# Attention into four experts on one core: order of the first chunks, places of the second batch's attention, and a last block in two column halves

## The chip, the cores and the metric

The kernel runs on one core of a Trainium2 chip. The metric is the time of one execution on the device in microseconds. The core's engines are TensorE (PE: matrix products into PSUM; PEld: its loading of the stationary operand), VectorE (DVE), ScalarE (ACT), GpSimd (POOL) and SyncE (SP). Here POOL and SP also issue the DMAs.

## The reference

Pooled attention for 8 batches of 8 heads, 576 tokens and 64 columns per head, then four experts on the 4608 tokens:

```
k_p, v_p = mean of k and v over groups of 8 tokens          # 72 keys per head
attn     = softmax(q @ k_p^T / sqrt(64))                    # per head
x        = attn @ v_p, heads side by side                   # [4608, 512]
p        = domain_probs / (sum over experts + 1e-9)
out      = sum over e of p[:, e] * (relu(x @ w1[e]) @ w2[e])  # w1 512x1024, w2 1024x512
```

All operands of the matrix products are bf16.

## The kernel before

**Chunks and steps.** The tokens are worked on in nine chunks of 512. Chunk c below 8 holds the first 512 tokens of batch c; chunk 8 holds the last 64 tokens of all batches. For every chunk there are four experts, so there are 36 steps (c, e), numbered s = 4c + e. In step s the hidden layer of (c, e) is made ("up") while the output of the step before, s - 1, is accumulated ("down").

**Forms of a step.** Some steps multiply plainly: `up_plain` makes 8 row blocks of the hidden layer, each with four matmuls of 512 columns into a PSUM bank `h_ps` and a relu on ScalarE; `down` makes four output blocks r of 128 tokens, each with 8 matmuls of 512 columns into a bank `o_ps`, and `merge` adds the block, times its probability, to `acc` (on VectorE, or on ScalarE for e = 0). The others use a Strassen form: seven half-size products in place of eight (`up_seven`, products of 256 columns into banks `g_ps`, with sums and relus on ScalarE (L691, L698) and VectorE (L695)); from step 7 on `up_down` uses it for up and down together. The Strassen forms need combinations of w1 (`combine_w1`), w2 (`combine_w2`), x (`forms_of`) and of the hidden layer (`sums_of`), most of them made on VectorE. Some overwrite a block that the plain form still needs, so they may only run once the last plain user is through.

**Order.** Every engine's queue is in the order in which the Python code runs; nothing is reordered by a scheduler. A counter `at` counts points: each call of `point()` runs what the dictionary `placed` holds for that number. `between(j, n)`, with j in 0, 1 and n in 0 to 3, makes one point, then a quarter of one half of the previous step's down products (3, 4, 5 and 4 matmuls), then pops one entry of the queue `forms_due` and makes a second point. A step without `up_down` so has 16 points; step 4 begins at point 64.

**Attention.** The attention of batch 0 (`attention_first`) runs at the start. That of batch 1 (`second_attention`) is placed at the points 42 to 64: its keys are folded on VectorE, transposed on TensorE (`second_keys`, L319), its queries are transposed in two halves (`second_queries`, L329), then come four groups of scores (`scores`, L272, followed by an exp on ScalarE, L276), the folding of the values, and four groups of contexts (`context`, L395), each followed on VectorE by a reciprocal and a division (`divide`, L376 and L377) and on SP by a DMA transpose (`turn`, L416) into `xT`. From batch 2 on `attention(c)` places the same work during chunk c for batch c + 1, with c = 1 for batch 2, and keys and queries are turned by DMA transposes (`keys`, `queries`). In `loads_wait` POOL waits for the transposed keys before it issues further loads.

**PSUM.** There are three pools: `psum_a` holds one tile of two banks, used in turn by scores, contexts and the transposes named above; `psum_h` and `psum_o` hold three banks each. A tile can be written again once its last reader is through.

**Places that the change touches.** `turn_here` (L423) turns x of batch 0 on TensorE: it takes a tile of `psum_a` for r = 0 and for r = 2, and r = 1 and 3 use that tile's other half. In step 4, (1, 0), the up products of chunk 1 are plain and alternate with the down products of (0, 3) in the second half of the step (L1006 to L1010). At the very end the step after the last one runs the down products of (8, 3), each block followed by an addition (L872) and, since chunk 8 gathers two batches per block, two stores of 64 rows (L888).

Of the kernel before, what the change touches and what calls it, by code (L numbers as in the profile page):

```python
# [13 lines left out]
BF16 = mybir.dt.bfloat16  # L14
F32 = mybir.dt.float32
# [3 lines left out]
def kernel(  # L19
# [10 lines left out]
    nc = tc.nc  # L30

    B, H, S, D = q.shape
# [78 lines left out]
    def load_q(b):  # L111
        q_sb = qpool.tile([P, H, NR, D], BF16, name="q_sb")
        nc.gpsimd.dma_start(
            out=q_sb[:].rearrange("p h r d -> p h (r d)"),
            in_=q[b, :, 0:NT, :].rearrange("h (p r) d -> p h (r d)", r=NR),
        )
        raws[("q", b)] = q_sb
# [22 lines left out]
    def load_v(b):  # L140
        load_kv(b, v, "vraw")
# [281 lines left out]
    def turn_here(b, r):  # L423
        if r == 0:
            state[("xT", b)] = xpool.tile([P, KC, NT], BF16, name="xT")
        if r % 2 == 0 or b:
            state["xt_ps"] = psum_a.tile([P, 2, KC, P], BF16, tag="a", name="xt_ps")
        xt_ps = state["xt_ps"][:, r % 2]
        flat = state.pop(("x", b, r))[:].rearrange("p a h d -> p (a h d)")
        for kc in range(KC):  # L430
            nc.tensor.transpose(xt_ps[:, kc, :], flat[:, kc * P:(kc + 1) * P], ident[:])
        nc.scalar.copy(out=state[("xT", b)][:, :, r * P:(r + 1) * P], in_=xt_ps)  # L432

    def rem_queries(i):
        q_rem = q_rems.pop(i)
# [80 lines left out]
    def second_attention():  # L516

        lo, hi = halves

        return {  # L520
            42: [lambda: fold_keys(1, lo)],
            44: [lambda: fold_keys(1, hi), lambda: load_k(2)],
            47: [second_keys],
            50: [lambda: second_queries(0)],
            51: [lambda: second_queries(1), lambda: load_q(2), lambda: load_q_rem(2)],
            53: [lambda: scores(1, 0)],
            55: [lambda: scores(1, 1)],
            56: [lambda: fold_values(1, lo)],
            57: [lambda: scores(1, 2)],
            58: [lambda: fold_values(1, hi)],  # L530
            59: [lambda: scores(1, 3)],
            60: [lambda: context(1, 0), lambda: turn(1, 0)],
            61: [lambda: context(1, 1), lambda: turn(1, 1)],
            62: [lambda: context(1, 2), lambda: turn(1, 2)],
            63: [lambda: context(1, 3), lambda: turn(1, 3)],
            64: [lambda: load_v(2)],
        }

    def attention(c):

        lo, hi = halves
        b = c + 1
        plan = {}

        def add(n, *what):
            plan.setdefault(n, []).extend(what)

        if c % 2:
            i = c // 2
            q_at = 15 if b < B else 2  # L550
            for n, piece in zip((0, 8, 11, 12), (rem_queries, rem_scores, rem_context, rem_turn)):
                add(q_at + n, lambda piece=piece: piece(i))
        parts = forms_of(b, nc.gpsimd)
        add(25, *parts)
        if b == B:
            return plan
        more, far = b + 1 < B, b + 2 < B
        if c == 1:
            add(0, lambda: queries(b), *key_parts(b)[:2])
            add(1, *key_parts(b)[2:])  # L560
            add(1, lambda: keys(b), lambda: loads_wait(b))
            add(1, lambda: (load_q(b + 1), load_q_rem(b + 1)))
            for pair in range(NPAIR):
                add(7 + pair, lambda pair=pair: scores(b, pair))
            for n, part in enumerate(value_parts(b)):
                add(6 + n, part)
            mixed = (11, 12, 13, 14)
        else:
            for pair in range(NPAIR):
                add(2 + 2 * pair, lambda pair=pair: scores(b, pair))  # L570
            for n, part in enumerate(value_parts(b)):
                add(4 + n, part)
            mixed = (9, 11, 12, 19)
        for n, r in zip(mixed, range(NR)):
            add(n, lambda r=r: context(b, r))
            add(n + 1, lambda r=r: turn(b, r))
        if more:
            add(4, lambda: load_half(b + 1, k, "kraw", 0))
            add(11, lambda: queries(b + 1))
            add(8, lambda: load_half(b + 1, k, "kraw", 1))  # L580
            add(16, *key_parts(b + 1))
            add(21, lambda: load_half(b + 1, v, "vraw", 0))
            add(27, lambda: load_half(b + 1, v, "vraw", 1))
            add(24, lambda: keys(b + 1))
        if far:
            add(28, lambda: (load_q(b + 2), load_q_rem(b + 2)))
        return plan
# [259 lines left out]

    def down(c, e, j, n):

        first = (0, 3, 7, 12, 16)  # L850
        for at in range(first[n], first[n + 1]):
            r, fc = 2 * j + at // FCH, at % FCH
            if fc == 0:
                sums[r] = psum_o.tile([P, DM], F32, name="o_ps")
            nc.tensor.matmul(  # L855
                sums[r][:], lhsT=hidden[(c, e)][:, fc, r * P:(r + 1) * P], rhs=w2_bf[:, e, fc, :],
                start=(fc == 0), stop=(fc == FCH - 1),
            )
            if fc == FCH - 1:
                if held is not None and r == NR - 1:  # L860
                    held.append(lambda: merge(c, e, r, sums[r]))
                else:
                    merge(c, e, r, sums[r])

    def merge(c, e, r, o_ps):
        prob = p_all[:, c * NR + r, e:e + 1]
# [10 lines left out]
            return  # L877
        store(c, r)

    def store(c, r):  # L880
        dst = accs[(c, r)][:]
        if c < B:
            rows = out[c * S:c * S + NT, :].rearrange("(p r) d -> p r d", r=NR)
            nc.sync.dma_start(out=rows[:, r, :], in_=dst)
        else:
            for bb in range(2):
                at = (2 * r + bb) * S + NT
                nc.sync.dma_start(out=out[at:at + REM, :], in_=dst[bb * REM:(bb + 1) * REM])  # L888

    zeros = x_rem[:, 0]  # L890
    pool_map = x_rem[0:FR, 1, 0:FT * SP].rearrange("p (r j) -> p r j", r=FT)
# [1 line left out]
    with tc.manual_schedule(engines={ENG.PE, ENG.DVE, ENG.Activation, ENG.Pool, ENG.SP}):  # L893
# [52 lines left out]
        for s in range(len(steps) + 1):  # L946
# [17 lines left out]
            if s == 1:  # L964
                w, u, x = combine_w2(0), combine_w1(0), forms_of(0)
                forms_due.extend([lambda w=w, u=u, n=n: (w[n](), u[n]()) for n in range(3)])
                forms_due.extend(nothing[:1] + combine_w1(2))
                for part in x[:3]:
                    part()
            elif s == 2:  # L970
                x[3]()
                forms_due.extend(nothing + combine_w1(3))
            elif s == 4:
                v2, x = combine_w2(1), forms_of(1)
                forms_due.extend(v2[:2] + combine_w1(1))
                forms_due.extend([lambda: (x[0](), x[1]()), lambda: x[2]()])
            elif s == 5:
                x[3]()
                forms_due.extend(u[3:] + nothing[:2] + combine_w2(2))
            elif s == 6:  # L980
                v3 = combine_w2(3)
                forms_due.extend(nothing[:1] + v3[:1] + nothing[:2] + v3[1:])
            elif s == 7:
                forms_due.extend(nothing[:1] + v2[2:3] + nothing[:3] + v2[3:])
            elif s == 8:
                forms_due.extend(nothing[:1] + w[3:])
            elif s == E * B + 1:
                reload_w2(E - 1)
            for j in range(2):
                if not live:  # L990
                    for n in range(4):
                        between(j, n)
                elif s == 0:
                    for i in range(4):
                        up_half(j, i)
                        if j == 0 and i in (1, 2):
                            turn_here(0, i + 1)
                        if j == 0 and i == 2:
                            norm_probs()
                        between(j, i)  # L1000
                elif s == 1:
                    for n in range(4):
                        between(j, n)
                    for n in range(4):
                        up_plain(c, e, [4 * j + n])
                elif s == E:  # L1006
                    for n in range(4):
                        between(j, n)
                        if j:
                            up_plain(c, e, [2 * n, 2 * n + 1])  # L1010
                elif splits(*steps[s - 1]):
                    up_down(c, e, j, *steps[s - 1])
                else:
                    up_seven(c, e, j, lambda n: between(j, n))
# [30 lines left out]
```

## Time and profile before

| what | value |
|---|---|
| median of three runs | 506.51 us (506.37 to 507.28) |
| profiled execution | 508.62 us |
| its span on the core | 506.9 us |
| TensorE busy | 494.3 us, 98% |
| VectorE, ScalarE, GpSimd busy | 70%, 57%, 35% |
| granted TensorE clock, mean | 0.997 |
| DMA | 41.90 MB, near full in the first 75 us, far less later |

The profile comes from one execution. A row of a timeline gives start and duration in us, engine, line, operation, output and inputs, and in brackets the idle time of the engine before it with the instruction that ended it. Matmuls overlap, so a row of several matmuls lasts about 0.16 us longer than the time until the next row can start. A granted clock of 0.50 means half speed of TensorE.

### The profile page before, as it was taken

What the parts mean: (1) busy time and instruction counts of PE and PEld (TensorE: products, weight loads), DVE (VectorE), ACT (ScalarE), POOL (GpSimd) and SP (SyncE); (2) the same over time, 40 slices, a digit from 0 to 9 for tenths busy, and PEclk for the clock granted to TensorE, in tenths of its full rate; (3) what the DMA queues carried; (4) which work ended last, traced back from release to release, by engine and by line L of the source; (5) the groups of instructions that cost most, each with busy time, mean ns of one, the idle gap of its engine ahead of it and who ended that gap; (6) DMA issues with size and microseconds to landing.
All of it is one profiled execution on the core that took longest, in us unless ns stands there. A gap on an engine that the chain in (4) does not pass through costs nothing.

```text
span 506.9 us, 10946 instructions
## 1 busy us (share of the span) xinstructions
PE 494.3 (98%) x4483; PEld 392.6 (77%) x4483; DVE 355.5 (70%) x650; ACT 287.6 (57%) x531; POOL 179.7 (35%) x165
## 2 busy tenths in 40 slices
PE   8899889999999999999999999999999999999996
PEld 3656544567788888888888888888888888888883
DVE  2363879678777776777777777777877767776674
ACT  2554352745676557665766576556655565556650
POOL 8372102135622671266226722661115111512110
PEclk9899999999999999999999999999999999999999
DMA  9999998893747346844773286343200110012003
GB/s 130 206 206 204 203 142 155 127 88 38 83 106 98 48 47 121 118 48 44 125 107 51 21 124 118 50 46 63 64 16 18 43 43 12 2 43 63 2 1 83
DMA packets 83506, 41.90 MB, mean 83 GB/s; under 512 B 46576, under 2 KB 78832, under 8 KB 83456
## 3 DMA queue, kind: packets, MB, share of 16 engines
q0 software_dynamic: 42112, 22.91, 35.4%
q1 hardware_dynamic: 41344, 18.29, 17.8%
q8 instruction: 35, 0.57, 0.5%
q14 instruction: 15, 0.12, 0.1%
HBM read 45.69 MB, written 9.44 MB: 109 GB/s over the span
## 4 chain that ended last, share of the span: by engine, by line
PE 90%; DVE 5%; DMA 1%; ACT 1%; issue 1%; POOL 1%; POOLq 0%; ACTq 0%
PE g_ps L647 38%; PE u_ps L769 35%; PE o_ps L855 8%; PE h_ps L665 3%; PE two L272 2%; PE h_ps L678 2%; PE two L395 1%; DMA q_sb<-in_q_dram 1%; DVE H_sb L695 1%; DVE x_tok L377 1%; DVE acc L872 1%; DVE acc L753 0%; ACT xT L432 0%; PE two L452 0%; POOL H_sb L107 0%
## 5 line engine op out<-in xcount | busy, mean ns | idle before, releaser
L647 PEld LDWEIGHTS <-w_bf 128*128 128x128 bf16 x1848 | 177.5, 98 | 27.8 <-issue 2.5
L753 DVE SCALAR_TENSOR_TENSOR acc<-u_ps,p_all,acc 128x512 f32<-128x512 f32 (+1 forms) x204 | 121.3, 594 | 77.0 <-ACT u_ps L806 72.7
L715 POOL TENSOR_TENSOR h_s<-H_sb,h_s 128x1024 bf16<-128x1024 bf16 x29 | 61.4, 2119 | 231.1 <-DVE h_s L714 231.1
L647 PE MATMUL g_ps<-xT,w_bf 128*128 128x256 bf16 x928 | 130.0, 273 | 0.0
L647 PE MATMUL g_ps<-xf,w_bf 128*128 128x256 bf16 x792 | 109.8, 272 | 0.6 <-ACT g_ps L790 0.4
L691 ACT COPY r<-g_ps 128x512 f32<-128x512 f32 x140 | 82.1, 586 | 46.4 <-PE g_ps L647 41.8
L695 DVE CUSTOM_DVE_ANT_0 H_sb<-g_ps,r 128x512 bf16<-128x512 f32 x140 | 96.4, 689 | 12.8 <-ACT r L691 8.2
L769 PEld LDWEIGHTS <-H_sb 128*128 128x128 bf16 x928 | 86.8, 98 | 18.2 <-DVE H_sb L713 4.7
L769 PE MATMUL u_ps<-w_bf,H_sb 128*128 128x256 bf16 x696 | 95.3, 273 | 0.4 <-DVE H_sb L713 0.3
L698 ACT ACTIVATE H_sb<-g_ps 128x512 bf16<-128x512 f32 x124 | 74.1, 597 | 20.6 <-PE g_ps L647 20.6
L769 PEld LDWEIGHTS <-h_s 128*128 128x128 bf16 x696 | 68.1, 98 | 7.9
L790 ACT COPY g_ps<-g_ps 128x512 f32<-128x512 f32 x58 | 33.1, 570 | 65.3 <-PE g_ps L647 65.3
L769 PE MATMUL u_ps<-w_t,h_s 128*128 128x256 bf16 x464 | 69.6, 273 | 0.0
L855 PE MATMUL o_ps<-w_bf,H_sb 128*128 128x512 bf16 x224 | 54.7, 379 | 0.0
L806 ACT COPY u_ps<-u_ps 128x256 f32<-128x256 f32 x58 | 20.7, 357 | 32.8 <-PE u_ps L769 32.6
L855 PEld LDWEIGHTS <-H_sb 128*128 128x128 bf16 x224 | 21.7, 98 | 18.9
L769 PE MATMUL u_ps<-w_t,H_sb 128*128 128x256 bf16 x232 | 35.0, 273 | 0.0
L769 PE MATMUL u_ps<-w_bf,h_s 128*128 128x256 bf16 x232 | 34.8, 273 | 0.0
L276 ACT ACTIVATE expT<-two 72x1024 bf16<-72x1024 f32 x28 | 28.5, 1017 | 4.0 <-PE two L272 4.0
L377 DVE TENSOR_TENSOR x_tok<-two,inv 128x512 bf16<-128x512 f32 x32 | 22.1, 692 | 1.1
L808 DVE TENSOR_SCALAR acc<-u_ps,p_all 128x512 f32<-128x512 f32 x14 | 10.5, 751 | 16.8 <-ACT u_ps L806 16.8
L794 ACT COPY u_ps<-u_ps 128x256 f32<-128x256 f32 x58 | 21.1, 363 | 0.0
(116 smaller groups left out, 433.0 us busy)
## 6 DMA issues: line engine op xcount, KB each, us to landing
out_dram<-acc SPq DMA_DIRECT2D x32, 256.0 KB, 2.4
w_bf<-in_moe_w_dram POOLq DMA_DIRECT2D x17, 256.0 KB, 10.1
w_bf<-in_moe_w_dram POOLq DMA_DIRECT2D x4, 1024.0 KB, 17.4
q_sb<-in_q_dram POOLq DMA_DIRECT2D x7, 512.0 KB, 10.0
raw_kv<-in_k_dram POOLq DMA_DIRECT2D x10, 288.0 KB, 6.6
raw_kv<-in_v_dram POOLq DMA_DIRECT2D x10, 288.0 KB, 6.6
raw_kv<-in_k_dram POOLq DMA_DIRECT2D x2, 576.0 KB, 14.8
w_t<-in_v_dram POOLq DMA_DIRECT2D x2, 576.0 KB, 13.7
```

The source lines that it names most:

```text
L276: nc.scalar.activation(out=state[("expT", b)][:, 2 * pair:2 * pair + 2].rearrange("j h r s p -> j s (h r) p"), in_=two[0:SP].rearrange("j ...
L377: nc.vector.tensor_tensor(out=x_tok[:], in0=c_ps[:, :, :, 0:D], in1=inv[:].unsqueeze(3).to_broadcast([P, 2, NPAIR, D]), op=ALU.mult,)
L647: nc.tensor.matmul(bank[:, t, :], lhsT=w1_bf[:, e, block, kc, lo:lo + P], rhs=x[:, kc, :], start=(first and t == 0 and kc == 0), stop=(t = ...
L691: nc.scalar.copy(out=r[:], in_=ps[:])
L695: nc.vector._custom_dve(TENSOR_ADD_SAT, out=out, in0=ps[:], in1=r[:], s0=BIG, s1=0.0)
L698: nc.scalar.activation(out=out, in_=ps[:], func=ACT.Relu)
L715: lambda: nc.gpsimd.tensor_sub(out=s4, in0=a12, in1=s2),
L753: nc.vector.scalar_tensor_tensor(out=acc, in0=ps, scalar=prob, in1=acc, op0=ALU.mult, op1=ALU.add,)
L769: nc.tensor.matmul(out, lhsT=lhs[0][:, lhs[1] + f, lhs[2]], rhs=rhs[0][:, rhs[1] + f, rhs[2]], start=(start and f == 0), stop=(f == FCH // ...
L790: nc.scalar.copy(out=s[:], in_=g[:])
L794: nc.scalar.copy(out=two[:, lo], in_=one[:, lo])
L855: nc.tensor.matmul(sums[r][:], lhsT=hidden[(c, e)][:, fc, r * P:(r + 1) * P], rhs=w2_bf[:, e, fc, :], start=(fc == 0), stop=(fc == FCH - 1),)
```

## The change

The change has six parts.

1. `turn_here`: each r takes a tile of one bank's half; r = 1 takes it from `psum_o`, the others from `psum_a`.
2. `second_attention`: keys of batch 1 move from point 47 to 49, the second half of the queries from 51 to 52 with the loads of q that follow, the first three groups of scores one point later, the contexts from 60, 61, 62, 63 to 61, 63, 65, 68, and the load of v of batch 2 to 69.
3. `attention(1)`: the transposes and folds of batch 2 begin two places (four points) later, its scores, values and contexts one place later.
4. Step 4: all down products of its second half come first, then all eight plain row blocks.
5. `forms_due`: the four combinations of w2 of expert 1 move from steps 4 and 7 to steps 7 and 8; in step 4 the combinations of w1 of expert 1 and the forms of x are queued later and two at a time.
6. End: the last block of (8, 3) is made in two halves of 256 columns, each with its own addition and store, and the stores of chunk 8 become one DMA per block (or half) in place of two.

```diff
     def turn_here(b, r):
...
-        if r % 2 == 0 or b:
-            state["xt_ps"] = psum_a.tile([P, 2, KC, P], BF16, tag="a", name="xt_ps")
-        xt_ps = state["xt_ps"][:, r % 2]
+        pool, tag = ((psum_o, "o_ps") if r == 1 else (psum_a, "a"))
+        xt_ps = pool.tile([P, KC, P], BF16, tag=tag, name="xt_ps")
...
-            47: [second_keys],
+            49: [second_keys],
             50: [lambda: second_queries(0)],
-            51: [lambda: second_queries(1), lambda: load_q(2), lambda: load_q_rem(2)],
-            53: [lambda: scores(1, 0)],
-            55: [lambda: scores(1, 1)],
-            56: [lambda: fold_values(1, lo)],
-            57: [lambda: scores(1, 2)],
-            58: [lambda: fold_values(1, hi)],
+            52: [lambda: second_queries(1), lambda: load_q(2), lambda: load_q_rem(2)],
+            54: [lambda: scores(1, 0)],
+            56: [lambda: scores(1, 1), lambda: fold_values(1, lo)],
+            58: [lambda: scores(1, 2), lambda: fold_values(1, hi)],
             59: [lambda: scores(1, 3)],
-            60: [lambda: context(1, 0), lambda: turn(1, 0)],
-            61: [lambda: context(1, 1), lambda: turn(1, 1)],
-            62: [lambda: context(1, 2), lambda: turn(1, 2)],
-            63: [lambda: context(1, 3), lambda: turn(1, 3)],
-            64: [lambda: load_v(2)],
+            61: [lambda: context(1, 0), lambda: turn(1, 0)],
+            63: [lambda: context(1, 1), lambda: turn(1, 1)],
+            65: [lambda: context(1, 2), lambda: turn(1, 2)],
+            68: [lambda: context(1, 3), lambda: turn(1, 3)],
+            69: [lambda: load_v(2)],
...
         if c == 1:
-            add(0, lambda: queries(b), *key_parts(b)[:2])
-            add(1, *key_parts(b)[2:])
-            add(1, lambda: keys(b), lambda: loads_wait(b))
-            add(1, lambda: (load_q(b + 1), load_q_rem(b + 1)))
+            add(2, lambda: queries(b))
+            add(2, *key_parts(b)[:2])
+            add(3, *key_parts(b)[2:])
+            add(3, lambda: keys(b), lambda: loads_wait(b))
+            add(3, lambda: (load_q(b + 1), load_q_rem(b + 1)))
             for pair in range(NPAIR):
-                add(7 + pair, lambda pair=pair: scores(b, pair))
+                add(8 + pair, lambda pair=pair: scores(b, pair))
             for n, part in enumerate(value_parts(b)):
-                add(6 + n, part)
-            mixed = (11, 12, 13, 14)
+                add(7 + n, part)
+            mixed = (12, 13, 14, 15)
...
     def down(c, e, j, n):
-        first = (0, 3, 7, 12, 16)
+        if (c, e) == (B, E - 1) and j and n:
+            if n == 1:
+                for lo in (0, TH):
+                    last_half(c, e, NR - 1, lo)
+            return
+        first = (0, 3, 7, 12, 16) if (c, e) != (B, E - 1) or j == 0 else (0, FCH)
...
+    def last_half(c, e, r, lo):
+        o_ps = psum_o.tile([P, DM], F32, tag="o_ps", name="o_ps")
+        cols = slice(lo, lo + TH)
+        for fc in range(FCH):
+            nc.tensor.matmul(
+                o_ps[:, 0:TH], lhsT=hidden[(c, e)][:, fc, r * P:(r + 1) * P],
+                rhs=w2_bf[:, e, fc, cols], start=(fc == 0), stop=(fc == FCH - 1),
+            )
+        dst = accs[(c, r)][:, cols]
+        add(dst, p_all[:, c * NR + r, e:e + 1], o_ps[:, 0:TH])
+        nc.sync.dma_start(out=rem_rows(r)[:, :, cols], in_=dst)
...
+    def rem_rows(r):
+        return out.rearrange("(b s) d -> b s d", s=S)[2 * r:2 * r + 2, NT:S]
...
-            for bb in range(2):
-                at = (2 * r + bb) * S + NT
-                nc.sync.dma_start(out=out[at:at + REM, :], in_=dst[bb * REM:(bb + 1) * REM])
+            nc.sync.dma_start(out=rem_rows(r), in_=dst)
...
             elif s == 4:
-                v2, x = combine_w2(1), forms_of(1)
-                forms_due.extend(v2[:2] + combine_w1(1))
-                forms_due.extend([lambda: (x[0](), x[1]()), lambda: x[2]()])
+                x = forms_of(1)
+                u1 = combine_w1(1)
+                forms_due.extend(nothing + [
+                    lambda: (u1[0](), u1[1]()), lambda: (u1[2](), u1[3]()), lambda: x[0](),
+                    lambda: (x[1](), x[2]()),
+                ])
...
             elif s == 7:
-                forms_due.extend(nothing[:1] + v2[2:3] + nothing[:3] + v2[3:])
+                v2 = combine_w2(1)
+                forms_due.extend(nothing[:1] + v2[:1] + nothing[:3] + v2[1:2])
             elif s == 8:
-                forms_due.extend(nothing[:1] + w[3:])
+                forms_due.extend(nothing[:1] + w[3:] + v2[2:3] + nothing[:2] + v2[3:])
...
                 elif s == E:
                     for n in range(4):
                         between(j, n)
-                        if j:
-                            up_plain(c, e, [2 * n, 2 * n + 1])
+                    if j:
+                        up_plain(c, e, range(FCH))
```

More of the change, by code (lines that the diff above doesn't have):

```diff
@@ L431, in turn_here @@
             nc.tensor.transpose(xt_ps[:, kc, :], flat[:, kc * P:(kc + 1) * P], ident[:])
-        nc.scalar.copy(out=state[("xT", b)][:, :, r * P:(r + 1) * P], in_=xt_ps)
+        nc.scalar.copy(out=state[("xT", b)][:, :, r * P:(r + 1) * P], in_=xt_ps[:])
     def rem_queries(i):
```

## The prediction

> **What bounds the kernel now.** I read the page first: engine shares, then the chain that ended last.
>
> ```profile
> PE 494.3 (98%) x4483; PEld 392.6 (77%) x4483; DVE 355.5 (70%) x650; ACT 287.6 (57%) x531; POOL 179.7 (35%) x165
> ...
> PE 90%; DVE 5%; DMA 1%; ACT 1%; issue 1%; POOL 1%; POOLq 0%; ACTq 0%
> ```
>
> TensorE carries nine tenths of the chain, and from 95 us to the tail the waits name four idle gaps of TensorE, none over 0.3 us. The change neither adds nor removes matrix work to speak of, so it can only win or lose in places where TensorE waits. The timeline of TensorE, searched for idle time, gives these places before 95 us; the number in brackets is the idle time and who ended it:
>
> ```profile
> 18.07 0.38 PE L431 MATMUL xt_ps<-ident,x_tok 128*128 128x128 bf16 x4 [0.41 <-ACT xT L432]
> ...
> 56.02 0.30 PE L319 MATMUL kpt_ps<-ident,kp 72*128 72x72 bf16 x4 [0.98 <-DVE kp L207]
> ...
> 60.33 0.61 PE L329 MATMUL qt_ps<-ident,q_sb 128*128 128x128 bf16 x8 [0.30 <-DVE qT L333]
> ...
> 72.35 0.43 PE L395 MATMUL two<-vp,expT 72*128 72x65 bf16 x8 [0.61 <-DVE x_tok L377]
> ...
> 73.84 0.43 PE L395 MATMUL two<-vp,expT 72*128 72x65 bf16 x8 [0.63 <-DVE x_tok L377]
> ...
> 75.30 0.43 PE L395 MATMUL two<-vp,expT 72*128 72x65 bf16 x8 [0.16 <-DVE x_tok L377]
> ```
>
> All of them lie where the diff works: transposes of batch 0 (18 us), keys and queries of batch 1 (56 to 60), its contexts (70 to 75). The last place is the end, where TensorE is done at 502.30 and the rest is one addition and two stores:
>
> ```profile
> 497.92 6.29 SPq L888 DMA_DIRECT2D out_dram<-acc  x8
> ...
> 502.33 0.75 DVE L872 SCALAR_TENSOR_TENSOR acc<-o_ps,p_all,acc 128x512 f32<-128x512 f32 x1 [0.98 <-PE o_ps L855]
> ```
>
> The windows view adds the granted clock, 0.50 from 19.0 to 22.4 us, where 16 products of 256 columns take 0.213 us each and not 0.109.
>
> **What the Trainium skill says.** "TensorE: Matmul & The Clock Gate", section "What's actually happening": after an idle window of about 3.4 us the clock is halved, and the windows run freely. The trace agrees (3.4 us at half clock after a stretch with many gaps). "PSUM — Partial Sum Buffer", section "Engine vs sequencer instructions": VectorE and ScalarE queues are strictly first in, first out. The trace agrees: at 58.40 two relu sums (L695) run back to back, the first behind two weight combinations. "DMA: Bandwidth & Descriptors", section "Anatomy of one DMA": about 2 us of a DMA are fixed. The trace agrees: 128 KB stores land 2.2 us after issue, 256 KB ones 2.3 to 2.4.
>
> **The change part by part.** Rows used: four 256-column products 0.44, a down product 0.216, a group of scores 0.34 plus 0.10 of delay ahead of it (61.65 + 5 x 0.216 = 62.73, but it starts at 62.82), a group of contexts 0.26, from one context to the next when VectorE is free 1.46 (73.84 to 75.30).
>
> *Start.* `turn_here` r=1 gets a bank of its own. Its four transposes start at 17.66, after the contexts, and not at 18.07; the first up product then starts at 18.70, not 19.13. **-0.4**. For r=2 and 3 nothing changes: they shared a bank before, and still take turns in one.
>
> *Keys and queries of batch 1.* `second_keys` moves behind eight products (0.87) and three down products (0.65), so to 54.75 + 1.52 - 0.4 = 55.9. The folded keys are ready at 55.96 - 0.4 = 55.56, so the 0.98 is gone. What is late next is the load of q of batch 1: issued at 35.97, it lands 21.8 later, at 57.8. TensorE would reach `second_queries` at 55.9 + 0.28 + 0.87 = 57.0 and waits until 57.85. Then 0.44 + 4 x 0.216 gives 59.15, eight products 60.02, where the second half needs the first half's copy. VectorE has no gap here: relu sums (58.40 + 1.28) and copy (0.68), all 0.4 earlier, end at 59.9. So the second half runs 60.02 to 60.46, and the five down products after it start at 60.46, not 61.65: **-1.19 with the start, -0.79 without**.
>
> *Contexts of batch 1.* Before, start minus nominal end of the work ahead: 0.30 (the last exp held the bank), 0.78, 0.78, 0.33 = 2.19. After, walking on from 60.46: scores 0 waits 0.1 for the query copy; scores 2 and 3 now have only 0.86 of products between them, and the 1.02 us exp plus the copy of g put ahead of it on ScalarE hold the bank, 0.43; each context has 1.1 to 1.6 of products to the next one, but VectorE also runs a merge (0.66) or relu sum (0.65) ahead of the divide: 0.44, 0.20, 0.42. Sum 1.59, **-0.60**.
>
> *25 down products, then all 32 up products.* Same matrix work, **0**. The up products need the four turned pieces of x: they landed at 77.6 to 79.2 before, behind the load of v of batch 2 (69.98 + 7.1 = 77.1). Now the last is issued near 76.8 and lands near 79.2, while TensorE gets there at 81.0. ScalarE's relu takes 0.60 per 0.865 of matmul. On SP's queue one output store now stands ahead of the transpose of q of batch 2 and a second one ahead of that of its keys (all four came after it before); by my walk the keys go out at 81.3 (81.75 before), and they are needed at 89.1. POOL's order is unchanged.
>
> *Next step (c=1, e=1).* Its first half now holds four exps, not three: four of 1.02, three copies of 0.59, one relu 0.60, two merges 0.69 = 7.8 of 8.3 us on ScalarE. The last exp ends about 97.5 where the first context of batch 2 is reached at 97.25: 0.3. Contexts 2 and 3 of batch 2 are now two points apart with a weight combination (0.68) ahead of the divide: 2.95 against 2.64, 0.3. Nothing there waited before. **+0.6**.
>
> *w2 combinations of expert 1* go from steps 4 and 7 to 7 and 8; used in step 10. Step 8 gets two VectorE instructions of 0.68; after the first VectorE had 2.3 us idle (to 143.54), the second delays the sums of the next step by 0.6. **0**, at most 0.3.
>
> *Tail.* 24 products of 512 and 16 of 256 take the same time. The last addition is 128x256: about 0.45 (1.01 for two at 494.02), not 0.75. The last block then goes out by one store, not two: the second was issued at 503.62. The final issue comes at 502.32 + 0.03 + 0.45 = 502.8: **-0.8**. Cover: the first half's addition and issue end at 502.4.
>
> Sum: -1.19 - 0.60 + 0 + 0.6 + 0 - 0.8 = **-2.0**. The profiled execution took 508.62 (span 506.90 and 1.72 around it), so 506.6 for the like. The three runs shown have a median of 506.51, 2.1 below the profiled one; the difference of 2.0 is carried to it: **504.5**.
>
> Bounds from both sides. Start with keys and queries: -0.2 if the loads, which run 90% of the time here, end the waits; -1.4 if q lands early. Contexts: 0 if merges fall badly, -1.5 if no divide is late. Next step: 0 to +1.2. Tail: -0.5 to -1.0. I take the walk's values since each comes from rows next to the place.
>
> **Rivals.** *Loads take the gain.* w2 of expert 2 lands at 54.6 and is wanted at 55.2, q lands at 57.8 and is wanted at 57.0: earlier TensorE meets them. For: DMA is busy throughout these 40 us. Against: VectorE sets the second half of the queries anyway. With -0.2 there and +1.2 in the next step: -0.2 - 0.6 + 1.2 - 0.8 = -0.4, 506.1.
>
> *The half-clock window goes away.* With 0.4 us less idling before 19 us the window may count as busy. 16 products x (0.213 - 0.109) = 1.7 more: 502.8. For: the idling is just what is shortened. Against: 0.4 of 3.4 us is little, and the runs shown may already lack it.
>
> *Slower: keys of batch 2 land late.* They are the one transfer that now waits behind two stores on SP, and scores of batch 2 stop TensorE for it. Price: in the trace a transpose that met a large load took 13.0 us to land (q at 96.47), against 2.7 for these keys. 81.3 + 13 = 94.3 against 89.1 is 5.2 lost: 509.7. It turns the sign to slower when the landing passes 92.1. Against: POOL's next loads wait for exactly this transpose (`loads_wait`), and v of batch 2 has landed by then.
>
> That the change doesn't do what it says is excluded: in the built program the 25 down products stand in a row ahead of the 32 up products, and the contexts are spread.
>
> **Numbers.** Forecast 0.60 (0.56 faster, 0.04 within), loads 0.16 (0.02 and 0.14), clock 0.14, late keys 0.10. A measurement of this kernel can tell about 0.2%, 1.0 us, from no change. Faster 0.72, same 0.18, slower 0.10. Range 502.7 to 506.2, from the clock rival to the loads rival; what lies outside is mainly the late keys.
>
> **What would show it.** Right: no wait at the key transposes; `second_queries` starts near 57.8; four context waits below 0.5 each; up products from about 81 to 88; a wait near 0.3 at the first context of batch 2; last store issued 0.5 after TensorE ends. Wrong: TensorE waiting for a DMA before the scores of batch 2; new gaps after 95 us; a different stretch at clock 0.5.

## The result and the profile after

The changed kernel takes 522.40 us (median of 4 runs, 522.03 to 523.06) and the kernel before 506.45 us beside it (506.37 to 507.28): a ratio of 1.031, with a 95% interval of 1.0295 to 1.033. The forecast was 504.5. The profiled execution took 522.65 us, with a span of 521.0. One of the 21 executions with two store queues (below), the profiled one, took 1024.85 us and is left out, so that tail is read from the timeline of the last experiment.

First the page of the changed kernel, engine shares and chain. TensorE is busy about as long as before (493.0 us), but its share has fallen from 98 to 95%, and 5% of the chain are now DMA:

```profile
PE 493.0 (95%) x4491; PEld 392.4 (75%) x4491; DVE 355.0 (68%) x651; ACT 287.2 (55%) x531; POOL 179.6 (34%) x165
...
PE 83%; DMA 5%; DVE 5%; ACT 2%; issue 1%; POOL 1%; POOLq 0%; ACTq 0%
```

Next the timeline of its end (start, duration, engine, line; in brackets the idle time and who ended it). The last down products run from 493.26, the last addition starts at 500.39 and takes 0.48, as the prediction said. Then comes what it did not say: the two issues of the last block take 10.00 us together on SP's queue, where eight took 6.29 before, and the span ends at 521.0, more than 20 us after TensorE:

```profile
493.26 5.34 PE L858 MATMUL o_ps<-w_bf,H_sb 128*128 128x512 bf16 x24
...
495.97 5.05 SPq L905 DMA_DIRECT2D out_dram<-acc  x3
...
500.39 0.48 DVE L751 SCALAR_TENSOR_TENSOR acc<-o_ps,p_all,acc 128x256 f32<-128x256 f32 x1 [0.39 <-PE o_ps L873]
501.12 10.00 SPq L879 DMA_DIRECT2D out_dram<-acc  x2
```

And the DMA view of the changed kernel from 503 to 517 us, fourteen microseconds in which no other engine computes (queue: packets, MB, share of the 16 DMA engines):

```profile
DMA packets 423, 0.71 MB, mean 51 GB/s; under 512 B 8, under 2 KB 147, under 8 KB 423
...
q1 hardware_dynamic: 423, 0.71, 13.2%
```

Four blocks of 256 KB leave at 51 GB/s, with 13.2% of the DMA engines busy: two of 16 are 12.5%. At that rate the whole 1.05 MB takes 20.6 us; in the kernel before it leaves from 498 us to the end at 506.9 with 50.8% of the DMA engines busy. That is where the loss lies.

Ahead of the tail the idle places of TensorE are these (timeline of the changed kernel, up to 75 us):

```profile
18.83 1.91 PE L676 MATMUL h_ps<-xT,w_bf 128*128 128x256 bf16 x16 [0.41 <-ACT xT L431]
...
54.31 0.81 PE L858 MATMUL o_ps<-w_bf,H_sb 128*128 128x512 bf16 x3 [0.39 <-DMA w_bf<-in_moe_w_dram]
...
57.04 0.62 PE L329 MATMUL qt_ps<-ident,q_sb 128*128 128x128 bf16 x8 [0.78 <-DMA q_sb<-in_q_dram]
...
71.50 0.43 PE L395 MATMUL two<-vp,expT 72*128 72x65 bf16 x8 [0.26 <-DVE x_tok L377]
...
74.45 0.43 PE L395 MATMUL two<-vp,expT 72*128 72x65 bf16 x8 [0.16 <-DVE x_tok L377]
```

The wait for the keys (0.98) is gone, those at the contexts have shrunk, and two waits for loads have come. The 16 products at 18.83 take 1.91 and not 3.48: this execution has no half-clock stretch, which was worth 1.57. From one landmark of TensorE to the next, both profiled executions:

| stretch, by the start of | before | after | change |
|---|---|---|---|
| first down products of step 2 | 42.60 | 40.74 | -1.86, of which -1.57 is the half-clock stretch |
| down products behind the queries of batch 1 | 61.65 | 59.68 | -0.11 more |
| products behind the 32 up products of (1,0) | 90.27, with 0.44 of scores ahead | 87.02 | -0.84 more |
| first row of 12 down products in step 7 (chain view) | 121.17 | 118.75 | +0.39 |
| last down products | 495.22 | 493.26 | +0.46 |
| end of the span | 506.9 | 521.0 | +16.06 |

The sum is 14.1, the difference of the spans; without the half-clock stretch it is 15.7, next to the 15.95 between the medians. So the body (all that lies ahead of the last down products) gains 0.4 us without that stretch, and the tail loses 16.1.

### The profile page after: what moved, and what is told of

It reads as the page before. It is cut to its first block, busy times and chain, and to the rows that moved or that the text cites. A ratio compares the mean times of both kernels' runs of the same rounds, so it can differ in the third digit from the quotient of the medians.

```text
span 521.0 us, 10962 instructions
## 1 busy us (share of the span) xinstructions
PE 493.0 (95%) x4491; PEld 392.4 (75%) x4491; DVE 355.0 (68%) x651; ACT 287.2 (55%) x531; POOL 179.6 (34%) x165
## 4 chain that ended last, share of the span: by engine, by line
PE 83%; DMA 5%; DVE 5%; ACT 2%; issue 1%; POOL 1%; POOLq 0%; ACTq 0%
PE g_ps L645 35%; PE u_ps L767 33%; PE o_ps L858 6%; DMA q_sb<-in_q_dram 5%; PE h_ps L663 2%; PE two L272 2%; PE two L395 1%; PE h_ps L676 1%; DVE acc L751 1%; DVE H_sb L693 1%; DVE x_tok L377 1%; DVE w_bf L636 0%; ACT r L689 0%; PE o_ps L873 0%; ACT xT L431 0%
## 5 line engine op out<-in xcount | busy, mean ns | idle before, releaser
L767 PEld LDWEIGHTS <-H_sb 128*128 128x128 bf16 x928 | 86.7, 98 | 18.3 <-DVE H_sb L711 4.9
L858 PE MATMUL o_ps<-w_bf,H_sb 128*128 128x512 bf16 x216 | 52.9, 379 | 0.4 <-DMA w_bf<-in_moe_w_dram 0.4
L858 PEld LDWEIGHTS <-H_sb 128*128 128x128 bf16 x216 | 20.6, 98 | 18.6 <-issue 1.2
```

What stands on the lines that cost most here:

```text
L767: nc.tensor.matmul(out, lhsT=lhs[0][:, lhs[1] + f, lhs[2]], rhs=rhs[0][:, rhs[1] + f, rhs[2]], start=(start and f == 0), stop=(f == FCH // ...
L858: nc.tensor.matmul(sums[r][:], lhsT=hidden[(c, e)][:, fc, r * P:(r + 1) * P], rhs=w2_bf[:, e, fc, :], start=(fc == 0), stop=(fc == FCH - 1),)
```

## Experiments

Two theories for the tail. **Few engines**: the store `rem_rows(r)` has two steps (batches) in its outermost dimension, and so runs on two DMA engines. **Column halves, or size**: the pieces of 1 KB rows, or 256 KB to two separate places, are slow by themselves. The median of the kernel before was 506.9, 507.13 and 506.91 beside the three sets of runs.

**Two stores again (first set).** In both places of the store:

```diff
-        nc.sync.dma_start(out=rem_rows(r)[:, :, cols], in_=dst)
+        for bb in range(2):
+            at = (2 * r + bb) * S + NT
+            nc.sync.dma_start(out=out[at:at + REM, cols], in_=dst[bb * REM:(bb + 1) * REM])
```

> The changed kernel, but each of the last chunk's blocks goes out by two stores of 64 rows again (one for each batch); the column halves of the last block stay, as two stores of 64x256 each. Theory 'few engines': the merged store, whose outermost DRAM dimension has two steps, is moved by two of the 16 DMA engines at 51 GB/s, and four of them (1 MB) take 20.5 us; with 64 rows outermost each store lands in about 2.2 us, TensorE's end is followed by about 3.3 us, and the time is 505.5 to 506.3 us, 16 us below the changed kernel. Rival 'column halves': the last block's pieces of 1 KB rows are what is slow, or the last additions; then the time stays above 515. Rival 'body': the time was lost before the tail; then it stays at 520 or more.

Measured: 507.46 us, ratio 1.0005 (0.9995 to 1.0015). Fifteen of the sixteen microseconds are back with the column halves still there; it is the merged store. The time is 1 us above the range expected, though. In the timeline of this kernel ten issues stand in SP's queue, and the last ends at 502.81, 2.2 us after the last addition (500.58):

```profile
495.68 4.56 SPq L909 DMA_DIRECT2D out_dram<-acc  x6
...
500.10 0.48 DVE L751 SCALAR_TENSOR_TENSOR acc<-o_ps,p_all,acc 128x256 f32<-128x256 f32 x1 [0.39 <-PE o_ps L873]
500.33 2.48 SPq L881 DMA_DIRECT2D out_dram<-acc  x4
```

**The kernel before with the merged store.**

```diff
-            for bb in range(2):
-                at = (2 * r + bb) * S + NT
-                nc.sync.dma_start(out=out[at:at + REM, :], in_=dst[bb * REM:(bb + 1) * REM])
+            rows = out.rearrange("(b s) d -> b s d", s=S)[2 * r:2 * r + 2, NT:S]
+            nc.sync.dma_start(out=rows, in_=dst)
```

> The kernel before, with one edit: the last chunk's blocks go out by one store of 2x64x512 each. Everything else, the order of the products and the one last block of 512 columns included, is as before. Few engines: four stores of 256 KB at 51 GB/s are 20.5 us from the first one's issue (near 488 to 489 us as in the changed kernel, or as much later as the kernel before's tail is), so 520 to 524 us. Column halves or body: 506 to 507.

Measured: 523.82 us, ratio 1.033 (1.0306 to 1.0346). This one edit makes the whole loss, without any of the rest. The issues by line (shortest/median/longest ns) grow from 0.5 to 4.9 us as the queue behind the two engines fills:

```profile
L887 SPq DMA_DIRECT2D out_dram<-acc x4: 520/1126/4895, 497.4 to 502.5; - x4
```

**The same bytes, the dimensions exchanged** ("rows first" below).

```diff
-        return out.rearrange("(b s) d -> b s d", s=S)[2 * r:2 * r + 2, NT:S]
+        return out.rearrange("(b s) d -> s b d", s=S)[NT:S, 2 * r:2 * r + 2]
```

> The changed kernel, with one store for a block as it is, but the two outer dimensions of its DRAM side exchanged: 64 rows by 2 batches by 512. Bytes, rows of 2 KB and number of stores are the same; two tokens' rows within a block are stored at each other's places, so this part of the output is permuted. Few engines: what counts is the outermost dimension, so 64 puts the store on 16 engines: it lands in 2.3 to 2.5 us and the time is 505.0 to 506.0, a little under the form with two stores. Rival 'size': a store of 256 KB to two separate places is slow whatever the order of its dimensions: 520 or more.

Measured: 505.55 us, ratio 0.9969 (0.9962 to 0.9977). One store for a block, 256 KB, 2 KB rows, two places: all as in the changed kernel, and 16.9 us faster. Size is out. DMA view of this kernel, from 493 to 507 us in 40 slices (busy tenths of the 16 engines, then GB/s), and its landing times:

```profile
DMA  0000000000089101970029970900000000000000
GB/s 0 0 0 0 0 0 0 0 0 0 0 316 398 35 0 59 421 269 0 0 94 410 366 255 12 339 24 0 0 0 0 0 0 0 0 0 0 0 0 0
...
out_dram<-acc SPq DMA_DIRECT2D x3, 256.0 KB, 2.4
out_dram<-acc SPq DMA_DIRECT2D x2, 128.0 KB, 2.1
```

**Four batches in a block.**

```diff
-        return out.rearrange("(b s) d -> b s d", s=S)[2 * r:2 * r + 2, NT:S]
+        b, s = 4 * (r // 2), NT + 32 * (r % 2)
+        return out.rearrange("(b s) d -> b s d", s=S)[b:b + 4, s:s + 32]
```

> The changed kernel, with one store for a block, but the block goes to 32 rows of four batches (4x32x512) in place of 64 rows of two; the remainder rows of the output are permuted by this. Few engines: four engines at 25.6 GB/s each, 102 GB/s; 256 KB take 2.56 us, four blocks 10.2 us from the first issue. The blocks come every 1.73 us, so each is late by 0.83 us more than the one ahead, and the end is about 2.56 us of the last pair after a queue of some 2.5 us: 507 to 511 us, far below the changed kernel and above the form on 16 engines. Rival 'any leading dimension under 16 is equally slow' (one engine pair, whatever the shape): 522. Rival 'size': 522 as well.

Measured: 512.7 us, ratio 1.011 (1.009 to 1.0125). The DMA view from 500 to 508 us has twice the rate and twice the share of the changed kernel, which fits four engines in place of two (no view names single engines, so their number is read from rate and share):

```profile
DMA packets 460, 0.80 MB, mean 100 GB/s; under 512 B 13, under 2 KB 125, under 8 KB 460
...
q1 hardware_dynamic: 460, 0.80, 26.3%
```

The time is above my range. The rate expected holds, but only from about 500 us; ahead of that the first store had moved at 13 to 50 GB/s for 2.6 us. Why one such store alone is below the rate of its engines stays open.

**The body alone (second set):** `down` and `store` as in the kernel before, the rest as changed.

> The changed kernel with the tail of the kernel before: one last block of 512 columns, two stores for each of the last chunk's blocks, as before. This is the body of the change alone. By the traces (start -0.4, keys and queries -0.1, contexts -0.8, next step +0.4, two weight combinations in step 8 +0.46, that is -0.45 in all) against those runs of before that have no half-clock stretch (506.7): 506.1 to 506.4. By the prediction's own terms for the body (-1.2): 505.5. Rival 'the late stores hid more': above 507.

Measured: 506.54 us, ratio 0.998 (0.9973 to 0.9988). That is 0.6 below the median of before in this set (507.13), and 0.2 below the lower of the two groups in which its runs lie (see below; 506.72). It is 0.1 above the range that the traces gave; their -0.4 is nearer than the prediction's own -1.2 for the body.

**The turns of batch 0 alone:** the kernel before with the new `turn_here`.

> The kernel before with only the edit in the turns of batch 0: the second turned block has a bank of its own. Theory 'half clock': the runs of before fall into two groups, 506.3 to 507.2 and 507.8 to 508.5, and the upper one (a third of them) has the half-clock stretch after 19 us, worth 1.7; the shorter gaps take it away in every run, so that the runs form one group at 506.0 to 506.7, and the profile shows the 16 products at 18.5 us in 1.9 us. Rival: the edit wins its 0.4 only, with a third of the runs still 1.7 higher, and medians differ by 0.4. Second rival: the loads at 54 and 57 us take up the 0.4: 506.6 with one group.

Measured: 506.78 us, ratio 0.9988 (0.998 to 0.9996). The 52 runs of before in this set lie in two groups, 29 from 506.27 to 507.28 and 23 from 507.80 to 508.47; the 21 runs of this kernel lie in one, from 506.00 to 507.42. All but one of the upper group had a granted clock of 0.997 or less, which is what 3.4 us at half clock leave of 505 us; in the lower one two of 29 had. The medians of the groups are 1.3 apart (508.03 and 506.72), a little less than the stretch's 1.57; why is open. In the timeline of the kernel with this edit alone the 16 products take 1.91 us, and the later waits are those of before, for VectorE and not for loads:

```profile
18.32 1.91 PE L677 MATMUL h_ps<-xT,w_bf 128*128 128x256 bf16 x16 [0.41 <-ACT xT L431]
...
53.76 0.30 PE L319 MATMUL kpt_ps<-ident,kp 72*128 72x72 bf16 x4 [0.97 <-DVE kp L207]
...
58.08 0.61 PE L329 MATMUL qt_ps<-ident,q_sb 128*128 128x128 bf16 x8 [0.30 <-DVE qT L333]
```

With the edit the upper group is gone. That its runs had the half-clock stretch is inferred from the clocks (though two of the 21 runs, at 506.45 and 506.53, also have 0.997) and from the timelines: the two without the edit, before and before with the merged store, take 3.48 and 3.49 us for the 16 products, the ten with it 1.91 each. The edit's 0.4 does not show against the lower group (506.72 to 506.78), and the second rival does not explain it: TensorE waits for no load at 54 or 57 us in this timeline. Where the 0.4 goes stays open.

**The w2 combinations put back** to steps 4 and 7, on top of the kernel with rows first (edit: the branches for steps 4, 7 and 8 of the diff, undone).

> The changed kernel with its store's DRAM side in the order 64 rows by 2 batches (as in the run with rows first, 505.55 us; two tokens' rows are exchanged within a block, so that part of the output is permuted), and the w2 combinations of expert 1 put back to steps 4 and 7. Theory 'step 8': the two combinations in step 8 delay the start of the next half by 0.21 and of the next step by 0.25; both go, and the time is 505.0 to 505.2. Rival: the same offsets come from elsewhere and stay: 505.5. Second rival: in step 4 the two early combinations stand ahead of the contexts' divides on VectorE and cost 0.3 to 0.6 there: 505.4 to 505.8.

Measured: 505.64 us, ratio 0.9965 (0.995 to 0.998); 505.55 with rows first alone. The second rival is right. The last context of batch 1 waits 0.74 in this timeline, and 0.16 in the one with rows first. The edit puts the w1 combinations and the forms of x back too, but what stands ahead of the divide on VectorE is the first w2 combination (L633, 0.68 us at 73.29):

```profile
74.87 0.43 PE L395 MATMUL two<-vp,expT 72*128 72x65 bf16 x8 [0.74 <-DVE x_tok L377]
```

So the move costs 0.46 in step 8 and saves 0.58 in step 4.

**Later loads.** On top of rows first, `load_v(1)`, `load_w2(3)` and both `load_q_rem` went from the start-up list to point 40 of `second_attention`.

> The changed kernel with the store of rows first (part of the output permuted, as there), and the loads of v of batch 1, of w2 of expert 3 and of the two q remainders (1.9 MB) issued at point 40, some 6 us later. Theory 'loads': TensorE waits at 54 us for w2 of expert 2 (0.42) and at 57 us for q of batch 1 (0.81) because these loads share the DMA engines with what is issued after them; with less behind them they land earlier, both waits go, and 0.7 to 1.1 us are won: 504.4 to 504.9. Rival 'VectorE': the copies behind the relu sums set the second half of the queries anyway, and only 0.2 to 0.4 are won: 505.2 to 505.4. Rival on the other side: v of batch 1 or w2 of expert 3 then lands too late, and the contexts wait: 506 or more.

Measured: 505.82 us, ratio 0.9972 (0.9963 to 0.9981). Inconclusive, because the edit moved nothing: POOL issues the load of v at 41.34 us here and at 40.57 with rows first. In both, its queue stood still for 3.93 us ahead of it until earlier loads had landed, and TensorE still waits for w2 (0.84) and q (0.69). It told me where to cut instead: ahead of the queries' load.

**Half of a load ahead (third set).** On top of rows first:

```diff
     def load_w2(e):
+        n = FCH // 2 if e == 2 else FCH
...
-            out=w2_bf[:, e], in_=...
+            out=w2_bf[:, e, 0:n], in_=rows[:, 0:n]
...
+        nc.vector.memset(w2_bf[:, 2, FCH // 2:FCH], 0.0)
```

> The run with rows first (505.55 us; part of the output permuted), with only half of expert 2's second matrix loaded (0.5 of 1 MB; the other half is set to zero by VectorE at the start, so expert 2's share of the output is left incomplete). The loads run at 202 GB/s without a pause from 5 to 60 us, so what lands after this matrix lands 2.6 us earlier. Theory 'loads': the waits of TensorE for w2 of expert 2 (0.42) and for q of batch 1 (0.81) both go, and with them 0.8 to 1.2 us: 504.3 to 504.8. Rival 'VectorE': the second half of the queries waits for its copy behind the relu sums instead, 0.3 of it: 504.8 to 505.1. Rival 'the waits named are not the cause': 505.4 or more.

Measured: 504.53 us, ratio 0.9952 (0.9938 to 0.9965), 1.0 below rows first. Neither wait is in the timeline any more, and what is left at the queries is 0.15 for VectorE's copy:

```profile
57.70 0.61 PE L331 MATMUL qt_ps<-ident,q_sb 128*128 128x128 bf16 x8 [0.15 <-DVE qT L335]
```

The loads had taken the gain at the keys and queries.

**Two queues for the stores,** with the reference's output kept:

```diff
-        nc.sync.dma_start(out=rem_rows(r)[:, :, cols], in_=dst)
+        for bb, queue in enumerate((nc.sync, nc.scalar)):
+            at = (2 * r + bb) * S + NT
+            queue.dma_start(out=out[at:at + REM, cols], in_=dst[bb * REM:(bb + 1) * REM])
```

> The changed kernel with two stores for each of the last chunk's blocks, 64 rows each as in the form before, but the two go out from two queues, SyncE's and ScalarE's (idle by then). Theory 'SP issues': the form with two stores on SP alone (507.46) is 1.9 above the form with rows first because ten issues of 0.5 to 0.8 us stand in one queue, the last ending 2.2 us after the last addition; with two queues the last two issues run side by side and the time is 505.3 to 505.9. Rival 'size of the transfer': 64-row stores of 1 KB rows are what is slow, and the time stays above 507.

Measured: 506.0 us, ratio 0.9978 (0.9972 to 0.9985), 0.1 above the range expected and 1.5 below the form with both stores on SP. The size of the transfer is the same, so the issues in one queue were the cost there.

**And the last two w2 combinations in VectorE's idle time:**

```diff
-                forms_due.extend(nothing[:1] + w[3:] + v2[2:3] + nothing[:2] + v2[3:])
+                forms_due.extend(nothing[:1] + w[3:] + nothing[:1] + [lambda: (v2[2](), v2[3]())])
```

> The kernel with two store queues, and the last two w2 combinations of expert 1 at the end of the first half of step 8, where VectorE idles for 1.96 us, in place of the third and sixth slot. Theory 'step 8': the delays of 0.21 and 0.25 go without the loss of 0.58 that these combinations had in step 4, and the time is 0.4 to 0.5 below that of the form with two queues, near 505.1. Rival: the next half's first addition or relu sum is then late instead: no difference.

Measured: 505.24 us, ratio 0.9966 (0.9953 to 0.9978): the best version that computes the whole reference, 1.7 us under the kernel before and 17 under the changed one. From the last context of batch 1 to the last down products it takes 492.13 - 73.79 = 418.34 us; with rows first, 492.90 - 74.08 = 418.82. The 0.48 matches the 0.46 of step 8. Against the median with two queues it is 0.76 less, 0.3 more than expected; why stays open. In its timeline the last issues stand side by side:

```profile
498.90 1.34 SPq L881 DMA_DIRECT2D out_dram<-acc  x2
498.90 1.43 ACTq L881 DMA_DIRECT2D out_dram<-acc  x2
```

From the start of the last down products to the end of the span, in the timelines of the eight kernels:

| tail | us | against before |
|---|---|---|
| before: 8 stores on SP | 11.68 | |
| body alone, same tail | 11.6 | -0.1 |
| column halves, 10 stores on SP | 12.6 | +0.9 |
| column halves, 5 on SP and 5 on ScalarE | 11.2 | -0.5 |
| column halves, merged, rows first | 10.8 | -0.9 |
| column halves, merged, four batches first | 17.8 | +6.1 |
| column halves, merged, two batches first (the change) | 27.7 | +16.1 |
| one block of 512, merged, two batches first | 27.5 | +15.8 |

## Why the prediction was wrong

**The tail: the failing step.** "The last block then goes out by one store, not two" was counted as one issue saved, and the whole tail as -0.8, bounded by -0.5 and -1.0. Measured: +16.1. The step took its price from rows of another shape. The stores of the trace before have 64 or 128 rows in their outermost dimension (landing in 2.2 to 2.4 us); a store of 2 x 64 x 512 was not in it, and the step put the cost of the new shape at nothing. The Trainium skill has a rule for it, in "DMA: Bandwidth & Descriptors", section "Why a DMA increments its semaphore by 16 and not by 1": the number of engines is the largest up to 16 that divides the slowest dimension, other than one of size 1, on both sides. Here these sizes are 2 in DRAM and 128 in SBUF, which gives 2. The runs agree: 51 GB/s and 13.2% for two, 100 GB/s and 26.3% for four, up to 421 GB/s in a slice for 64. I took the time of a landing from the old stores and did not look up the new shape. The rest of the step was right: with 64 rows outermost the tail measures -0.9, and the last addition takes 0.48 where 0.45 was said.

The second form of this error showed in the first experiment. Ten issues of 0.57 us on one queue cost +0.9 in the tail, although each store landed as fast as before: column halves double the last block's issues (with merged stores it is one for each half, so two as before, not one), and the issues go on for 2.2 us after the last addition.

**Start: right, and the clock rival with it.** From the turns at 17.11 (17.33 after) to the first up product there were 2.02 us and are 1.50, against -0.4 predicted. (Up to step 2 only 0.3 of these 0.5 show in the profiled execution, whose first turns came 0.22 later.) The rival with 0.14, that the half-clock stretch goes, came true, with 1.57 in the profiled execution (1.7 was the price for 16 products; 15 of them ran at half clock); the 21 runs of the turns alone have no run in the upper group, where 23 of 52 were before. As the rival itself said, the runs shown may lack it, and the median of before mostly does. Of what the prediction says of the clock, the trace shows the length, 3.4 us. It shows no idle window ahead of it: TensorE was busy for 2.18 of the 3.4 us before 19.0.

**Keys and queries: -0.79 predicted, -0.11 measured.** The key wait went as said, but in place of one wait for VectorE at the second half TensorE waits for loads: it is idle 0.39 for w2 of expert 2, which the sum had not counted, and 0.78 for q. Counted as the walk counts (start less the nominal end of the work ahead), that is 0.55 and 0.94; the walk had 0 and 0.85, and this is 0.64 of the 0.68 that is missing. TensorE was 1.86 earlier and not 0.4, since the half-clock stretch was gone too, and q landed only 0.8 earlier (about 57.0 for 57.8). That is the mechanism of the rival "loads take the gain", and cutting 0.5 MB ahead of them gives 1.0 us.

**Contexts: -0.60 predicted, -0.84 measured.** Three idle gaps of 0.28 (at the last scores, for the exp), 0.26 and 0.16 remain. Counted as the walk counts, the waits are 0.46 at the scores and 0.43, 0.14 and 0.33 at the contexts, where it had 0.43, 0.44, 0.20 and 0.42: mechanism and sizes were right. **Next step: +0.6 predicted, +0.39 measured.** It is nearly all at the fourth context of batch 2, which starts 0.37 late (0.20 of it idle); the first, where 0.3 was expected, has no wait.

**w2 combinations: 0, at most 0.3, predicted; +0.46 measured in step 8.** The prediction named the 2.3 us of VectorE's idle time as cover for the first. The first is issued before that idle time starts, ahead of a relu sum which the next half waits for, and costs 0.21. The second costs 0.25, not 0. What it missed on the other side is that to leave step 4 is worth something: there they cost the last context 0.58.

**Keys of batch 2 late: no.** After 57 us the waits of TensorE name no DMA.

Summed without the half-clock stretch, the body gives -0.4 where the prediction had -1.2 (the difference of 0.8 is 0.7 at the loads, 0.46 in step 8 and 0.1 at the start, less 0.2 each at the contexts and the next step), the tail +16.1 where it had -0.8. Only the last has the sign wrong, and it decides.

## What to carry to other kernels

When two DMAs are merged into one, the access pattern changes, and with it the number of engines that carry it: read the outermost dimension on both sides before counting the issue saved, and put the rows, not the groups, outermost (the form measured here writes two tokens' rows to each other's places, so the rows of the block would have to be laid out to fit). The Trainium skill has this as a rule ("DMA: Bandwidth & Descriptors", section "Rules for kernel authors": an outermost dimension under 16 confines the whole DMA to at most that many engines), and the profiles here show it as a low, even share of the DMA engines (13.2% and 26.3%) while no other engine computes. At the end of a kernel, count the issues in the last queue too; a second, idle queue took 1.5 us off here.

## What the runs showed of the hardware

One DMA engine carried about 25 GB/s of these stores, an estimate from 51 GB/s with two and 100 GB/s with four. The issue of a store on SP took about 0.54 us with 64 rows outermost and up to 4.95 us with two engines; with four it stayed at 0.54 to 0.70 us, although the last issue ended at 501.6 us and the span at 511.2. So a long issue went with a backlog here, but a short one does not exclude it. A store alone on four engines began at less than its rate (13 to 50 GB/s for 2.6 us). And with the gaps of TensorE ahead of 19 us shorter by 0.5 us, none of 21 runs lay in the upper group, where 23 of 52 had; from 15.6 to 19.0 us TensorE was busy for 2.18 us in the timeline with the half-clock stretch and for 2.47 us in the one of the turns alone.
